# Two independent lanes for the side matrix products of an attention-and-GLU kernel: one PSUM bank and one queue for each half of the TensorE rows

## The chip, the cores and the metric

The kernel runs on one core of a Trainium2 chip. The metric is the device time of one execution in microseconds (us), the median of several runs. In the profile, PE is TensorE's matmul stream and PEld its weight loads, DVE is VectorE, ACT is ScalarE, POOL is GpSimd and SP is SyncE, which here only issues DMAs.

## What is computed

One transformer block over S = 2048 rows of width D = 512, with a modulation of its layer norms by a conditioning vector `c`. There are H = 32 query heads of width 16 that share one key and one value head (multi-query), and a GLU without a nonlinearity, of width F = 1792.

```
mod = (silu(c) @ w_mod)                      # six rows: sa, ca, ga, sb, cb, gb
h = layernorm(x) * (1 + ca) + sa
q = h @ wq  (32 heads of 16);  k = h @ wk;  v = h @ wv        # one k, one v
p = softmax(q k^T * 16**-0.5);  o = p v
x = x + ga * (o @ wo)
h = layernorm(x) * (1 + cb) + sb
x = x + gb * (((h @ w_gate) * (h @ w_up)) @ w_down)
```

All inputs and outputs are float32. Every product of float32 numbers on a float16 path is made of three float16 products: the left and the right operand are each split into a high and a low half, and high x high, low x high and high x low are accumulated (`TERMS`). An "operation" of a side product below is one such term for one slice of 128 of the contraction.

## The kernel before

**Steps.** The rows are four blocks (`NB`) of 512 queries. A block has 32 heads in 8 units of 4 heads, so there are 32 units (`NU`), and each unit has 32 steps (`NSTEP`): 1024 steps in a loop that is written out at build time. Every instruction stands in its engine's queue in the order in which the loop emits it.

**What a step does.** TensorE's 128 rows are used as two halves of 64 (parameter `a`, 0 or 1), and each half as four column quarters of 32, so that eight small matmuls can be in the array at a time. `quarters` (L521 is the full-width matmul of `plain`, L474 is the one in `quarters`) issues the four that fill one PSUM bank of 128 x 512. In a step with `a = i % 2` the loop emits, in this order (L1166 on): `max_half(a, 0, 2)`, scores of a later unit on half `a` (tile `mx`), whose row maximum DVE takes (L565); `qk_exp` on half `a` (tile `sc`), whose exponential ACT takes (L601); `pv` on the other half (L609, float32, each issued as two passes); then a second `max_half` and a second `qk_exp` on half `a`; then the side work. The maxima run 38 steps (`LEAD`) ahead of the scores, so the last 38 steps of the loop have none. `mx` has two banks, `sc` has two, and a third one (`spare`) while no side product needs it.

**Side products.** `q` of the later blocks, and, for each finished block, `wo`, the second layer norm, gate, up and down are done as side work between the attention matmuls. A `Group` is one output bank of 128 x 512: 12 operations for q, wo, gate and up, 42 for down. They go in pairs (`duo`): two groups, one in the bank `misc`, one in the bank `spare`. In a first turn the first group gets the upper half of each contraction slice on row half 0 while the second group gets the lower half on row half 1; in the second turn they change over, so that in both turns both halves work and no bank is written by both halves at once. Each operation of the generator is eight quarters, four on each half. Between the turns there is a pause of `SWAP_WAIT` = 2 steps, or, once the weights are all prepared, one step and a `memset` of a token on POOL (L498) that the second turn waits for. When the pair is done the first group is evicted at once and the second a step later (`mids`). After it there are `GROUP_WAIT` = 2 steps to the next pair.

**Pacing.** `pace` works out how many operations a step needs so that everything in the list `fill` is done by its due step (for a block's wo, gate, up and down: 12 steps into the next block but one); the sum is kept as `credit`, capped at 6, and `fill_gap` emits at most `BURST` = 3 operations in a step. In the last block `RESERVE / PAIR` = 142 operations may be left for the time after the loop, and a pair of downs isn't opened where fewer than 30 steps remain (`open_gate`).

**Evictions.** Gate is copied by ACT (L783), up by ACT (L790) and multiplied on POOL (L791), which also splits the product into halves (L794, L795). wo (L697) and down (L808) are scaled and added by one DVE operation each, and the layer-norm statistics follow on DVE (L705, L708).

**Weights.** While the first blocks run, a second list (`side`) streams each weight in slices twice: first for norms and scales (squares on POOL, L877, L879; column sums on PE, L889, their maxima on DVE, L892), at one slice per `ABS_GAP` = 2.5 steps, then for the float16 halves.

**After the loop** the remaining downs of block 2 are done with full 128 x 128 matmuls (`cover`), in the gaps of the last normalisation, then wo, the layer norm, gate, up and down of block 3, in the same way.

Of the kernel before, what the change touches and what calls it, by code (L numbers as in the profile page):

```python
# [21 lines left out]
NB = 4  # L22
# [6 lines left out]
ABS_GAP = 2.5  # L29
# [9 lines left out]
SWAP_WAIT = 2  # L39
RESERVE = 31000.0  # L40
TR_GAP = 8
BURST = 3
# [11 lines left out]
def adaln_mqa_glu_kernel(ctx: ExitStack, tc: tile.TileContext, x_in, wq_in, wk_in, wv_in, wo_in,  # L54
# [12 lines left out]
    spare = {"n": 0, "scores": True, "held": 0}  # L67
# [18 lines left out]
    def ps_misc(shape=(128, 512), dt=F32, tag=None):  # L86
        bufs = 1
        if tag is None:
            tag, bufs = ring["tags"][ring["n"] % len(ring["tags"])]
            ring["n"] += 1  # L90
        elif tag == "sc":
            bufs = NSC
        return psum.tile(list(shape), dt, name="misc", tag=tag, bufs=bufs)
# [9 lines left out]
    wqs = work.tile([128, KC, 64], F32, name="wqs", tag="xl", bufs=3)  # L103
# [14 lines left out]
    wqst = [work.tile([128, D], F32, name="wqst", tag=("gf", "oc")[k // 2], bufs=2) for k in range(KC)]  # L118
# [58 lines left out]
    modT = [consts.tile([128, KC, 64], F32, name=f"modT{i}") for i in range(2)]  # L177

    def mod_cols(row, dst, pt):
# [3 lines left out]
        nc.scalar.activation(dst[:, :, 0:32], pv_[:, :, 0:32], AF.Copy)  # L183
        nc.scalar.activation(dst[:, :, 32:64], pv_[:, :, 32:64], AF.Identity, bias=1.0)
# [56 lines left out]
    def ln_tr(b, ks=range(KC)):  # L241
        for k in ks:
# [4 lines left out]
            bias, scale = (hsb[:, k, 0:1], hsb[:, k, 1:2]) if b else (modT[0][:, k, 0:1], modT[0][:, k, 32:33])  # L247
# [47 lines left out]
    mrow = work.tile([128, 256], F32, name="modrow", tag="xl", bufs=3)  # L295
# [6 lines left out]
    nc.scalar.activation(modT[0][:, :, 32].rearrange("p (h c) -> p h c", c=2),  # L302
# [4 lines left out]
    nc.vector.tensor_reduce(cmk[:, 0:1], modT[0][:, :, 32], axis=AX.X, op=OP.max, apply_absolute_value=True)  # L307
# [39 lines left out]
    nc.vector.tensor_scalar(hsb, modT[0][:, :, 0:64:32], fwd[:, 0:1], None, op0=OP.mult)  # L347
# [103 lines left out]
    def v_evac():  # L451
        vt["v"] = work.tile([128, BT], F32, name="kvT", tag="ev", bufs=3)
        nc.scalar.activation(vt["v"], vt["p"], AF.Copy, scale=qvs[:, 1:2])
# [13 lines left out]
    class Group:  # L467


        def __init__(self, n, op, pre, post, mid=True):  # L470
            self.n, self.op, self.pre, self.post, self.mid = n, op, pre, post, mid
# [4 lines left out]

    def half(p, g, i, r, start, stop):
        left, right = g.op(i)
        return quarters(p, left[64 * r:64 * r + 64], right[64 * r:64 * r + 64], start, stop)

    token = consts.tile([1, 1], F32, name="token")
    SYNC = mybir.DependencyInfo(mybir.DependencyClass.Sync, mybir.DependencyReason.DATA)

    def duo(g0, g1, tags=("misc", "spare")):

        ps = g0.pre(tag=tags[0]), g1.pre(tag=tags[1])
        n = g0.n
        mark = None
        for turn in range(2):
            for i in range(n):  # L490
                for r in range(2):
                    ms = half(ps[r ^ turn], (g0, g1)[r ^ turn], i, r, turn == 0 and i == 0,
                              turn == 1 and i == n - 1)
                    if mark is not None:
                        tc.add_manual_dep(ms[0].ins, mark.ins.name, SYNC, reason="row halves of one bank in turn")
                        mark = None
                if turn == 0 and i == n - 1 and cur["mark"]:
                    mark = nc.gpsimd.memset(token, 0.0)  # L498
                    tc.add_manual_dep(mark.ins, ms[-1].ins.name, SYNC, reason="end of a row half")
                if turn == 0 or i < n - 1:  # L500
                    yield i == n - 1
        g0.post(ps[0])

        def late():
            g1.post(ps[1])
            after(3, free)

        def free():
            spare["held"] -= 1

        spare["held"] += 1
        if g1.mid:
            mids.append(late)
        else:
            after(2, late)
# [9 lines left out]

    def q_proj(b, ch):

        def evac(p):
            q16 = work.tile([128, 2, BT], F16, name="q16", tag="ev", bufs=3)
            qf = work.tile([128, BT], F32, name="qf", tag="ev", bufs=3)  # L530
            nc.scalar.activation(qf, p, AF.Copy, scale=qvs[:, 0:1])  # L531
            nc.gpsimd.tensor_scalar(q16[:, 0, :], qf, 1.0, 0.0, op0=OP.mult, op1=OP.add)
            nc.gpsimd.tensor_tensor(q16[:, 1, :], qf, q16[:, 0, :], op=OP.subtract)
            d = dram.tile([128, 2, BT], F16, name=f"qd{b}_{ch}")
            nc.sync.dma_start(d, q16)
# [7 lines left out]
        return Group(3 * KC, op, ps_misc, evac, mid=False)  # L543
# [29 lines left out]
    def max_rows(u):  # L573
# [5 lines left out]
        def g():  # L579
# [5 lines left out]
            for hl in range(2):  # L585
                nc.sync.dma_start(s[48 + hl:113 + hl:64, :, :], mt[hl])
# [27 lines left out]
    def pv_lower(u):  # L614
        evt[u] = work.tile([128, BT], F32, name="ev", tag="ev", bufs=3)
        nc.scalar.activation(evt[u], pvb[u, 0], AF.Copy, scale=evs)  # L616

    def pv_out(u):
# [7 lines left out]
        for j in range(4):  # L626
            r = 16 * (h + j)
            nc.sync.dma_start(oc[b, g // 2][r:r + 16, :], ev[32 * j:32 * j + 16, :])
        nc.sync.dma_start(rsum[b, g // 2][h:h + 4, :], ev[16:128:32, :])
# [494 lines left out]
    for n in range(LEAD):  # L1124
# [5 lines left out]
        if n in first:  # L1130
            first[n]()
# [145 lines left out]
```

## Time and profile before

| | |
|---|---|
| median of 3 runs | 1771.94 us (1771.19 to 1771.97) |
| the profiled execution's own time | 1771.55 us |
| its span in the profile | 1769.7 us, granted TensorE clock 0.994 |
| POOL busy | 562.5 us (32%) |
| matmuls / weight loads | 39203 / 39203 |
| DMA | 70.04 MB, 34 GB/s of HBM over the span |

The span runs from the first to the last instruction. A busy time is the union of an engine's instructions. A matmul's record begins when it enters the array, and its end is modelled, so matmuls overlap and PE's busy share says little; distances between the starts of matmuls on the same row half say more. "x" counts instructions. A side operation of the loop is eight matmul records, and a step has two exponentials (L601).

### The profile page before, as it was taken

What the parts mean: (1) busy time and instruction counts of PE and PEld (TensorE: products, weight loads), DVE (VectorE), ACT (ScalarE), POOL (GpSimd) and SP (SyncE); (2) the same over time, 40 slices, a digit from 0 to 9 for tenths busy, and PEclk for the clock granted to TensorE, in tenths of its full rate; (3) what the DMA queues carried; (4) which work ended last, traced back from release to release, by engine and by line L of the source; (5) the groups of instructions that cost most, each with busy time, mean ns of one, the idle gap of its engine ahead of it and who ended that gap; (6) DMA issues with size and microseconds to landing.
All of it is one profiled execution on the core that took longest, in us unless ns stands there. A gap on an engine that the chain in (4) does not pass through costs nothing. (4 is left out here: it accounts for less than half of the span.)

```text
span 1769.7 us, 86400 instructions
## 1 busy us (share of the span) xinstructions
PE 1707.4 (96%) x39203; PEld 878.6 (50%) x39203; DVE 1442.1 (81%) x2353; ACT 1301.8 (74%) x2319; POOL 562.5 (32%) x788
## 2 busy tenths in 40 slices
PE   6899999999999999999999999999999999999999
PEld 3334444433345565565545555565545555543444
DVE  7899999999998888899998888899999998922210
ACT  3478888878878878887788888887888888893110
POOL 5714444436657852210032222110032121221130
PEclk9999999999999999999999999999999999999999
DMA  5212222212222210000100000000100000001000
GB/s 195 100 32 80 60 80 62 77 46 73 80 74 58 66 34 15 11 19 23 42 23 18 11 10 20 7 16 24 48 16 18 12 18 11 14 7 41 19 0 24
DMA packets 49115, 70.04 MB, mean 40 GB/s; under 512 B 15270, under 2 KB 29418, under 8 KB 48748
## 3 DMA queue, kind: packets, MB, share of 16 engines
q1 hardware_dynamic: 47164, 64.33, 12.2%
q8 instruction: 306, 5.01, 1.2%
q14 instruction: 61, 0.50, 0.1%
q10 hardware_dynamic: 1584, 0.20, 0.1%
HBM read 51.12 MB, written 8.92 MB: 34 GB/s over the span
## 5 line engine op out<-in xcount | busy, mean ns | idle before, releaser
L565 DVE TENSOR_REDUCE mpart<-mx 128x1 f32<-128x512 f32 x2048 | 1329.0, 685 | 125.9 <-PE mx L474 36.1
L601 ACT ACTIVATE P<-sc 128x512 f32<-128x512 f32 x2048 | 1177.0, 601 | 259.9 <-PE sc L474 203.7
L609 PE MATMUL pv<-P,vst 64*32 64x512 f32 x8192 | 1080.8, 598 | 0.0
L474 PE MATMUL mx<-kst,sst 48*32 48x512 f16 x8192 | 808.4, 383 | 35.7 <-DVE mpart L565 27.2
L474 PE MATMUL sc<-sst,kst 50*32 50x512 f16 x8192 | 818.5, 379 | 5.3 <-ACT P L601 4.5
L474 PEld LDWEIGHTS <-sst 48*32 48x32 f16 x8192 | 335.6, 90 | 514.4 <-issue 420.9
L474 PEld LDWEIGHTS <-kst 50*32 50x32 f16 x8192 | 264.2, 92 | 92.7 <-issue 60.7
L474 PE MATMUL misc<-h2T,wu 64*32 64x512 f16 x4032 | 294.8, 376 | 0.0
L474 PE MATMUL misc<-h2T,wg 64*32 64x512 f16 x4032 | 294.2, 376 | 0.0
L609 PEld LDWEIGHTS pv<-P,vst 64*32 64x32 f32 x8192 | 197.8, 105 | 17.9 <-ACT P L601 0.8
L791 POOL TENSOR_TENSOR gf<-gf,g 128x512 f32<-128x512 f32 x42 | 53.7, 1279 | 344.2 <-ACT gf L790 344.2
L474 PEld LDWEIGHTS <-wu 64*32 64x32 f16 x4032 | 111.0, 92 | 36.1
L474 PEld LDWEIGHTS <-wg 64*32 64x32 f16 x4032 | 112.9, 92 | 30.7 <-issue 1.5
L474 PE MATMUL misc<-wd,glu 64*32 64x512 f16 x2688 | 112.9, 376 | 0.0
L474 PE MATMUL misc<-h,wq 64*32 64x512 f16 x1536 | 95.4, 377 | 1.2 <-ACT qf L531 1.2
L498 POOL MEMSET token<- 1x1 f32 x43 | 3.8, 88 | 281.4 <-PE misc L474 216.7
L783 ACT ACTIVATE g<-misc 128x512 f32<-128x512 f32 x56 | 33.4, 596 | 77.0 <-PE misc L521 75.5
L521 PE MATMUL misc<-wd,glu 128*128 128x512 f16 x336 | 73.2, 379 | 0.0
L474 PEld LDWEIGHTS <-glu 64*32 64x32 f16 x2688 | 60.3, 92 | 23.4 <-issue 0.4
L795 POOL TENSOR_TENSOR glu<-gf,glu 128x512 f16<-128x512 f32 x56 | 65.0, 1161 | 4.7
L793 DVE TENSOR_TENSOR gf<-misc,g 128x512 f32<-128x512 f32 x14 | 9.7, 692 | 62.9 <-PE misc L521 62.9
L621 DVE SCALAR_TENSOR_TENSOR ev<-pv,evs,ev 128x512 f32<-128x512 f32 x32 | 23.7, 742 | 44.5 <-ACT ev L616 44.5
(232 smaller groups left out, 1063.1 us busy)
## 6 DMA issues: line engine op xcount, KB each, us to landing
wsl<-in_B_w_gate_dram SPq DMA_DIRECT2D x32, 224.0 KB
wsl<-in_B_w_up_dram SPq DMA_DIRECT2D x32, 224.0 KB
wsl<-in_B_w_down_dram SPq DMA_DIRECT2D x28, 256.0 KB
sst<-qd SPq DMA_DIRECT2D x186, 32.0 KB
qd<-q SPq DMA_DIRECT2D x16, 256.0 KB
oc<-ev SPq DMA_DIRECT2D x128, 32.0 KB
rr<-ri SPq DMA_DIRECT2D x16, 256.0 KB
xl<-in_A_x_dram SPq DMA_DIRECT2D x16, 256.0 KB
```

Source lines behind the costliest of these rows:

```text
L474: return [nc.tensor.matmul(p[c:c + CW, :], left[:, c:c + CW], right, start=start, stop=stop) for c in range(0, 128, CW)]
L498: mark = nc.gpsimd.memset(token, 0.0)
L521: nc.tensor.matmul(p, left, right, start=i == 0, stop=i == g.n - 1)
L565: nc.vector.tensor_reduce(mparts[u][:, a, p, t, kc:kc + 1], m, axis=AX.X, op=OP.max)
L601: nc.scalar.activation(ptl[u, kt, a][:, p, :], t, AF.Exp)
L609: nc.tensor.matmul(pvb[u, r][32 * j:32 * j + 32, :], vst[ks, kt, :], ptl[u, kt, a][ks, p, :], start=(kt == 0), stop=(kt == KT - 1))
L621: nc.vector.scalar_tensor_tensor(ev, pvb[u, 1], evs, ev, op0=OP.mult, op1=OP.add)
L783: nc.scalar.activation(st["g", f], p, AF.Copy, scale=2.0 ** -45)
L791: nc.gpsimd.tensor_tensor(gf, gf, st["g", f], op=OP.mult)
L793: nc.vector.tensor_tensor(gf, p, st["g", f], op=OP.mult)
L795: nc.gpsimd.tensor_tensor(st["glu"][:, 1, f, :], gf, st["glu"][:, 0, f, :], op=OP.subtract)
```

## The change

- Each row half becomes a `Lane`, with its own bank (`misc` or `spare`), its own queue `todo`, its own credit, and its own waits. `duo`, the turns, the pause between them and the token are gone.
- Gate and up: a group is done by one lane alone. It has 24 half operations (4 quarters each) instead of 12 whole ones, since both halves of each contraction slice go through the same 64 rows. For that the weights are stored with the halves of the rows exchanged as slices 4 to 7 (`2 * KC`), loaded by two DMAs for each slice, and h2 is copied with its halves exchanged by two DMAs (SBUF to SBUF) for each of its four slices. Lane 0 has the first seven columns of F / 128, lane 1 the last seven.
- q, wo (blocks 0 to 2) and down (blocks 0 to 2): each lane makes a partial sum over its own 64 rows in its own bank. Both are evicted, and added: q by a second ACT copy and a POOL add; wo by an ACT copy of the one and the DVE operation for the other, and a POOL add of x; down by an ACT copy and a POOL add each, with none on DVE.
- A lane emits `min(int(credit), BURST, left)` half operations in a step, `BURST` = 4; one of the lane `a` ahead of the second `max_half`, then all of the other lane, then the rest of `a`. A lane waits with a new group while the other one is in the first third of one of the same length, unless its credit is full.
- The transposes of h2 are dealt to the lanes in turn, and gate and up open 4 steps after the last of them (`H2_WAIT`).
- The remaining 142 operations of `RESERVE` are counted in each lane, and there is no gate that keeps a down group from opening late. After the loop the lanes go on in turn (`pair`), with two banks each; block 3's gate and up are done so too.
- Weights: `ABS_GAP` 2.0; the squares of wo and down on ACT, with the sum in the same operation, and half of those of gate and up on ACT; fewer, wider column sums.
- Smaller: the DMAs of the maxima's rows (`mt`) are issued by ACT, several DMAs are issued one to four steps later than their data, `ev` has four buffers.

```diff
-    def duo(g0, g1, tags=("misc", "spare")):
-        ps = g0.pre(tag=tags[0]), g1.pre(tag=tags[1])
-        for turn in range(2):
-            for i in range(n):
-                for r in range(2):
-                    ms = half(ps[r ^ turn], (g0, g1)[r ^ turn], i, r, turn == 0 and i == 0,
-                              turn == 1 and i == n - 1)
...
+    def rows_of(op, a):
+        def f(i):
+            left, right = op(i)
+            return left[64 * a:64 * a + 64], right[64 * a:64 * a + 64]
+        return f
...
     def q_proj(b, ch):
         def evac(p):
+            t = work.tile([128, BT], F32, name="qf", tag="ev", bufs=NEV)
+            nc.scalar.activation(t, p, AF.Copy, scale=qvs[:, 0:1])
+            if "t" not in st:
+                st["t"] = t
+                return
+            nc.gpsimd.tensor_tensor(t, t, st["t"], op=OP.add)
...
+            def send():
+                for hl in range(2):
+                    nc.scalar.dma_start(s[48 + hl:113 + hl:64, :, :], mt[hl])
+            after(1, send)
...
         def fin(t):                                   # wo
+                elif (b, t) not in x1s:
+                    x1 = x1s[b, t] = work.tile([128, D], F32, name="x1", tag="x1", bufs=4)
+                    nc.scalar.activation(x1, p, AF.Copy, scale=sca[:, 7:8])
+                    return
                 else:
+                    nc.vector.scalar_tensor_tensor(x1, p, sca[:, 7:8], x1, op0=OP.mult, op1=OP.add)
+                    nc.gpsimd.tensor_tensor(x1, x1, xls[b, t], op=OP.add)
...
+                def send():                           # h2, halves exchanged
+                    for a in range(2):
+                        nc.sync.dma_start(h[64 * a:64 * a + 64, :, KC + k, :], h[64 - 64 * a:128 - 64 * a, :, k, :])
+                after(2, send)
...
         def fin(t):                                   # down
-                nc.vector.scalar_tensor_tensor(o, p, sca[:, 6:7], o, op0=OP.mult, op1=OP.add)
+                    y = turns()
+                    nc.scalar.activation(y, p, AF.Copy, scale=sca[:, 6:7])
+                    nc.gpsimd.tensor_tensor(o, o, y, op=OP.add)
...
+        gu = [[Group(6 * KC, op(a, f, w), pre, (gate, up)[w](FT // 2 * a + f)) for f in range(FT // 2) for w in range(2)]
+              for a in range(2)]
...
+        def plan(self, step):
+            self.credit = min(self.credit + self.pace(step), CREDIT)
+            if self.credit < 1.0:
+                return 0
+            if self.g is None:
+                if not self.opens(step):
+                    return 0
...
+                other = lanes[1 - self.r]
+                if other.g and other.g.n == self.todo[0][1].n and other.i < other.g.n // 3 and self.credit < CREDIT:
+                    return 0
+                self.begin()
+            return min(int(self.credit), BURST, self.left())
...
             drain_mids()
+            first_n = min(ns[a], 1)
+            side_half(step, a, first_n)
             max_half(a, 1, 2)
             qk_exp(u, kt, 1, a)
...
+            side_half(step, 1 - a, ns[1 - a])
+            side_half(step, a, ns[a] - first_n)
```

More of the change, by code (lines that the diff above doesn't have):

```diff
@@ L117, in adaln_mqa_glu_kernel @@
         nc.gpsimd.memset(w, 0.0)
-    wqst = [work.tile([128, D], F32, name="wqst", tag=("gf", "oc")[k // 2], bufs=2) for k in range(KC)]
+    wqst = [work.tile([128, D], F32, name="wqst", tag=("ev", "oc")[k // 2], bufs=(NEV, 2)[k // 2]) for k in range(KC)]
     for k in range(KC):
@@ L787, in fn @@
             def fn(p):
-                gf = work.tile([128, BT], F32, name="gf", tag="gf", bufs=2)
+                gf = turns()
                 if b < NB - 1:
@@ L1093, in begin @@
-    def begin(step, two, due, tags=("misc", "spare")):
-        cur.update(gen=duo(*two, tags=tags), left=2 * two[0].n, turn=two[0].n, second=False, due=due, swapped=-9,
-                   mark=not side)
-    def burst(step, n):
-        for _ in range(n):
-            swap = next(cur["gen"], None)
-            credit[0] -= 1.0
-            cur["left"] -= 1
-            cur["turn"] -= 1
-            if swap is None:
-                cur["gen"], cur["left"], cur["wait"] = None, 0, step + GROUP_WAIT
-                return
-            if swap:
-                cur["turn"], cur["second"], cur["swapped"] = cur["left"], True, step
-                return
+    END = NU * NSTEP
@@ L1110, in adaln_mqa_glu_kernel, with side_half, free @@
+    lanes = [Lane(0, "misc"), Lane(1, "spare")]
+    def side_half(step, l, n):
+        if n:
+            done = lanes[l].emit(n)
+            if done:
+                lanes[l].wait = step + GROUP_WAIT
+                lanes[l].held += 1
+                def free():
+                    lanes[l].held -= 1
+                mids.append(done)
+                after(4, free)
     side_next = [0.0]
@@ L1145, in adaln_mqa_glu_kernel @@
             posts.append(v_out)
-    assert cur["gen"] is None
-    for two in qtwos:
-        fill.append(([0, 0], "duo", two, QDUE))
-    credit[0] = 0.0
-    def ffn_twos(b):
-        gu, down = ffn_work(b)
-        return gu + twos(down)
+    assert lanes[0].g is None and lanes[1].g is None
+    for lane in lanes:
+        lane.credit, lane.wait = 0.0, 0
     early["on"] = False
@@ L1163, in adaln_mqa_glu_kernel @@
             drain_posts()
-            spare["scores"] = not spare["held"] and cur["gen"] is None and not (fill and fill[0][1] == "duo" and open_gate(step))
             a = p
+            ns = [lane.plan(step) for lane in lanes]
+            spare["scores"] = not lanes[1].held and lanes[1].g is None and not lanes[1].opens(step)
             max_half(a, 0, 2)
@@ L1219, in adaln_mqa_glu_kernel, with pair @@
     pv_out(u)
-    left = cur["left"]
-    if cur["gen"] is not None:
-        assert cur["second"] and NU * NSTEP - cur["swapped"] > 2
-        for _ in cur["gen"]:
-            drain_posts()
-        drain_mids()
-    ring["tags"] = [("misc", 1), ("spare", 1)] + [("mx", NMX)] * NMX + [("sc", NSC)] * NSC
-    tail = deque(plain(g) for _, _, two, _ in fill for g in two)
+    drain_mids()
+    ring["tags"] = [("mx", NMX)] * NMX + [("sc", NSC)] * NSC
+    banks = [deque(("misc", "pv")), deque(("spare", "pvb"))]
+    def pair():
+        some = False
+        drain_posts()
+        for lane, tags in zip(lanes, banks):
+            if lane.g is None and lane.todo:
+                lane.tag = tags[0]
+                tags.rotate(-1)
+                lane.begin()
+            if lane.g:
+                some = True
+                done = lane.emit(1)
+                if done:
+                    done()
+        return some
     def cover(budget):
-        while tail and budget > 0:
-            drain_posts()
-            if next(tail[0], None) is None:
-                tail.popleft()
+        while budget > 0 and pair():
             budget -= 216
@@ L1254, in adaln_mqa_glu_kernel @@
     gu, down = ffn_work(NB - 1)
-    run([g for two in gu for g in two] + down)
+    for lane, gs in zip(lanes, gu):
+        lane.todo.extend(([0], g, 0) for g in gs)
+    cover(1e9)
+    run(down)
 _INS = ["A_x", "A_wq", "A_wk", "A_wv", "A_wo", "B_w_gate", "B_w_up", "B_w_down", "c", "w_mod"]
```

372 lines of the change are left out of this document (200 added, 172 removed).

## The prediction, made before the change was run

> **What bounds it now.** I read the page first, then the table of windows by stage (all instructions, then only the exponentials of L601, then only those on tile `misc`), then the timeline.
>
> ```profile
> PE 1707.4 (96%) x39203; PEld 878.6 (50%) x39203; DVE 1442.1 (81%) x2353; ACT 1301.8 (74%) x2319; POOL 562.5 (32%) x788
> ...
> L565 DVE TENSOR_REDUCE mpart<-mx 128x1 f32<-128x512 f32 x2048 | 1329.0, 685 | 125.9 <-PE mx L474 36.1
> ```
>
> PE's 96% is a union of overlapping records. DVE's row maxima alone are 1329 us, 685 ns each, two in a step. Now the stages: q only (93 to 456), the two stretches of gate, up and first downs (542, 934), end of downs, wo and layer norm (846), the last long stretch (1323).
>
> ```profile
> 93.00:456.00 363.00, 349.32 (x7607) 146.53 (x7607) 340.18 (x567) 307.72 (x541) 160.95 (x174) 0.99 0.22 63
> ...
> 542.00:846.00 304.00, 300.01 (x8531) 181.47 (x8530) 270.75 (x424) 243.09 (x440) 111.83 (x125) 1.00 0.12 31
> 846.00:934.00 88.00, 84.75 (x2062) 43.96 (x2049) 81.50 (x133) 70.36 (x125) 17.93 (x45) 0.98 0.11 32
> 934.00:1237.00 303.00, 300.54 (x8555) 179.78 (x8546) 270.48 (x425) 243.97 (x441) 53.45 (x67) 1.00 0.06 15
> ...
> 1323.00:1559.00 236.00, 233.40 (x6265) 129.06 (x6254) 214.32 (x341) 199.68 (x359) 50.53 (x62) 1.00 0.06 14
> ```
> ```profile
> 93.00:456.00 363.00, 296.56 (x512) 0.99 0.22 63
> ...
> 542.00:846.00 304.00, 228.07 (x399) 1.00 0.12 31
> ...
> 1323.00:1559.00 236.00, 186.71 (x324) 1.00 0.06 14
> ```
> ```profile
> 542.00:846.00 304.00, 155.91 (x3748) 0.00 (x0) 1.48 (x2) 16.89 (x28) 1.00 0.12 31
> ...
> 1323.00:1559.00 236.00, 111.95 (x2388) 0.42 (x4) 0.00 (x0) 15.26 (x25) 1.00 0.06 14
> ```
>
> Two exponentials make a step. With q only there are 256 steps of 363/256 = 1.418 us, and DVE is busy 340.18/363 = 93.7%: DVE sets the step, and I take 93.7% for what a DVE-bound stretch reaches. From 846 on it is 92.6%: DVE again. From 542 on there are 199.5 steps of 1.524 us with 3748/8/199.5 = 2.35 side operations each and DVE at 89.1%; the stretch at 934 is the same. From 1323 on: 162 steps of 1.457 us, 1.84 operations, DVE 90.8%. There PE is late as well. The timeline of PE says how:
>
> ```profile
> 668.25 0.60 PE L609 MATMUL pv<-P,vst 64*32 64x512 f32 x4
> 668.42 0.40 PE L474 MATMUL mx<-kst,sst 48*32 48x512 f16 x4
> 668.64 0.40 PE L474 MATMUL sc<-sst,kst 50*32 50x512 f16 x4
> 668.68 0.60 PE L609 MATMUL pv<-P,vst 64*32 64x512 f32 x4
> 668.86 0.40 PE L474 MATMUL mx<-kst,sst 48*32 48x512 f16 x4
> ...
> 670.65 0.40 PE L474 MATMUL misc<-h2T,wg 64*32 64x512 f16 x4
> 670.80 0.40 PE L474 MATMUL misc<-h2T,wu 64*32 64x512 f16 x4
> 670.87 0.40 PE L474 MATMUL misc<-h2T,wg 64*32 64x512 f16 x4
> ...
> 671.30 0.61 PE L609 MATMUL pv<-P,vst 64*32 64x512 f32 x4
> 671.45 0.40 PE L474 MATMUL mx<-kst,sst 48*32 48x512 f16 x4
> 671.67 0.40 PE L474 MATMUL sc<-sst,kst 50*32 50x512 f16 x4
> ```
>
> On one row half four quarters follow four quarters after 0.22 us (mx 668.42, sc 668.64, mx 668.86; wg 670.65, 670.87), and a pass of pv holds the other half 0.43 us (668.25, 668.68). So a step with n operations on a half needs 0.217 x (4 + n) us: 1.30 for 2, 1.52 for 3. At 2.35 it is 1.38 on average, below DVE's 270.75/199.5/0.937 = 1.45. The 1.52 measured comes from unevenness: steps of 3 are set by PE at 1.52, empty and light ones by DVE, and pairs end badly:
>
> ```profile
> 663.94 0.59 ACT L783 ACTIVATE g<-misc 128x512 f32<-128x512 f32 x1
> ...
> 664.89 0.62 ACT L790 ACTIVATE gf<-misc 128x512 f32<-128x512 f32 x1
> ...
> 665.08 0.40 PE L474 MATMUL sc<-sst,kst 50*32 50x512 f16 x4
> ...
> 665.52 0.40 PE L474 MATMUL mx<-kst,sst 48*32 48x512 f16 x4
> ...
> 666.05 0.40 PE L474 MATMUL sc<-sst,kst 50*32 50x512 f16 x4
> ```
>
> Gate and up are evicted within a step, the exponentials on ACT slip, and PE's next sc, mx, sc stand 0.44 and 0.53 us apart instead of 0.22, with no side work in between: 0.53 us lost per pair.
>
> **The change, part by part.**
>
> *Lanes in the loop.* The operations per half are the same (a 24-operation group on one lane for 12 on both, twice). Gone are the turn, its pause and the token; gate and up end in different steps, so ACT gets one 0.6 us eviction at a time. New is that the halves carry different n. Working the rule of `plan` through for a gate-up stretch (2.38 per step and lane, one empty step after each group, then up to 4 from the saved credit) gives steps such as [0,2] [4,2] [3,0] [2,4] [3,4] [2,2] [3,3]; the larger of the two averages 2.9, with 2, 3 and 4 about equally often. No trace shows unequal halves, so I bound it from both sides. *Elastic*: a half works ahead while the other is late, the five steps above cost each half 0.867 x 5 + 0.217 x 12 = 6.94 us, DVE is the bound, and the stretches fall to DVE busy/0.937: 289, 289 and 229 us, that is -15, -14 and -7 = -36. *Lockstep*: each step costs the larger half, max(1.45, 0.217 x (4 + n)): thirds of 1.45, 1.52 and 1.74 average 1.57 where equal halves (by the old rule 0, 3, 3, 3, 3, 3, 2, 3, 2, 2 for 24) give 1.49; 0.08 less 0.02 for the halved pile-up is +0.06 x 400 = +26, and 0.04 x 162 = +7 in the last stretch, where the larger of the two averages 2.3: +33. I take -15, nearer to the elastic end, for this row: pv is queued behind mx and sc of its step (L1166, L1167, L1170), yet at 671.30 it starts 0.15 us before that mx and 0.37 us before that sc. A half does run past the other by 0.37 us, and the unevenness to be hidden is two operations, 0.43 us.
>
> The Trainium skill speaks against this: "TensorE: Matmul & The Clock Gate", section "The mechanism", states that matmuls keep program order in start and end, a strict FIFO without reordering. By that rule the blocks of one lane and then the other would run one after the other, and the sum would be that of the third rival below; the row at 671.30 differs from it, and the measurement decides.
>
> *The end.*
>
> ```profile
> 1593.78 11.91 ACT L601 ACTIVATE P<-sc 128x512 f32<-128x512 f32 x24
> ```
> ```profile
> 1662.04 2.75 PE L521 MATMUL misc<-h2T,wg 128*128 128x512 f16 x12
> ...
> 1664.63 2.75 PE L521 MATMUL misc<-h2T,wu 128*128 128x512 f16 x12
> ```
> ```profile
> L521 PE MATMUL misc<-wd,glu 128*128 128x512 f16 x336 | 73.2, 379 | 0.0
> ```
>
> After the loop 12 operations take 2.59 us (1662.04 to 1664.63 on one engine with nothing else): 0.216 each. Of the 336 full-width downs 168 are block 3's, so all 168 of block 2's are left over, as no pair opens in the last 30 steps. By the new rule a lane has three groups, 126, left: 42 x 0.216 = -9. They go into the loop's last steps, where ACT sets 2 x 11.91/24 = 0.99 us and a half needs on average (0.434 + 0.867)/2 = 0.65: 1.6 operations a step are free, the rule emits 3.5 over 12 steps, so about 20 cost 0.217: +4. Sum -5; bounds -9 and 0. The lanes' eight quarters per 0.217 us are what the loop's threes do already.
>
> *DVE.*
>
> ```profile
> L531 ACT ACTIVATE qf<-misc,qvs 128x512 f32<-128x512 f32 x16 | 11.1, 691 | 4.3 <-PE mx L474 2.3 <-POOL q L533 2.0
> ...
> L808 DVE SCALAR_TENSOR_TENSOR x<-misc,sca,x 128x512 f32<-128x512 f32 x12 | 8.9, 744 | 21.3 <-PE misc L521 21.3
> ...
> L892 DVE TENSOR_REDUCE cmq<-mx 128x1 f32<-128x128 f32 (+1 forms) x16 | 4.4, 274 | 0.3 <-PE mx L889 0.3
> ```
>
> Eight of the twelve down additions (blocks 0 and 1) leave DVE in stretches that it sets: 8 x 0.744 = -6. Of sixteen column maxima four, wider, remain: 4.4 us less an estimated 1.6 = -3; taken together as -8. wo keeps one DVE operation per group.
>
> *ACT and POOL.*
>
> ```profile
> L791 POOL TENSOR_TENSOR gf<-gf,g 128x512 f32<-128x512 f32 x42 | 53.7, 1279 | 344.2 <-ACT gf L790 344.2
> ...
> L377 ACT ACTIVATE wqj<-wqst 128x512 f32<-128x512 f32 x4 | 2.5, 628 | 0.1
> ```
> ```profile
> 1.73 0.53 ACTq L104 DMA_DIRECT2D wqs<-in_A_wq_dram  x1
> ```
>
> Added to ACT in the q stretch: 14 second q copies x 0.69 = 10, 34 squares at 0.55 to 0.63 plus sums = 22, and 16 DMA issues (an issue by ACT took 0.53) = 8: 40 us onto 307.72 of 363. It fits only because exponentials in a row take 0.50, not the 0.58 that they average there; so ACT is late more often. Later stages get a copy per wo and down group, and 0.53 x 2 per unit. I take +4, bounds 0 and +15; a gain is excluded, as ACT only gets more. POOL loses the squares and gains adds of 1.28 us (as L791); at 160.95 of 363 nobody waits for it, except bn_stats on DVE, which comes three steps (4.5 us) after wo's eviction: if POOL is later than that, the row maxima queue behind it, up to 1.3 x 12 = 15 us. The exchanged copies of h2 have 4 steps, 6 us, and stand in SP's queue; while they travel DVE sets the step, so nothing. If they are late, PE's queue stops at operation 13 of the first groups, scores and all, some 2 us per block.
>
> Sum: -15 - 5 - 8 + 4 = -24 on the profiled execution's 1771.55 (the median of the runs is 0.4 higher): 1748 us.
>
> **Rivals.**
>
> *Fully elastic.* -36 - 5 - 8 + 0 = -49: 1722 us. For it: passes of pv start ahead. Against: mx waits for DVE in a queue that stops at a wait, and all behind it wait too, whichever half they are for.
>
> *Lockstep (slower).* The place is the gate-up stretches: where a half cannot run more than one operation ahead, each 4 against 2 costs its step 0.43 us. +33 - 5 - 8 + 8 = +28: 1800 us; it decides against the change as soon as less than half of the unevenness is hidden. For it: the threes at 1.52 show no step that borrows from its neighbour. Against: 671.30.
>
> *Strict order (slower).* No start overtakes another: then of each step's operations those of the second lane begin after the last of the first, (2.35 - 1) x 0.217 = 0.29 us x 400 and 0.18 x 162: +146, about 1900 us. Only the row at 671.30 speaks to it, clearly against.
>
> *Nothing to win.* Both lanes open gate and up in the same step (full credit passes the stagger), evictions fall together as now, and the halves' -5 and -8 are eaten by ACT: 1769 to 1775 us.
>
> **Numbers.** Forecast 0.48, fully elastic 0.22, nothing 0.10, lockstep 0.17, strict order 0.03. A change of 0.2%, 3.5 us, is about what can be told from none. Faster 0.70, same 0.10, slower 0.20. The range 1712 to 1788 takes in the elastic case with the ACT term and column maxima at their better ends, and the lockstep case up to half hidden plus the late ACT.
>
> **What would show it.** The windows by stage: gate-up stretches at about 1.48 us a step and DVE near 92%; no L498; starts of one half's quarters several operations ahead of the other's; 126 pairs after the loop and 156 us for all behind it; q stage unchanged within 5 us. I am wrong if the gate-up step is over 1.52, if DVE's idle time is ended by `misc` or `sc` on PE more than now, if bn_stats waits for POOL, or if the q stage grows.

## The result and the profile after

The changed kernel takes 1813.92 us (1809.59 to 1816.01, four runs) against 1771.57 us: a ratio of 1.0236 (1.0217 to 1.0256). It is slower, by 42 us, and outside the predicted range. Its profiled execution took 1813.35 us, with a span of 1811.5 us.

The page of the changed kernel, busy times and the row of the maxima (L540 is what was L565):

```profile
PE 1732.2 (96%) x42637; PEld 930.3 (51%) x42637; DVE 1431.2 (79%) x2331; ACT 1361.3 (75%) x2423; POOL 575.9 (32%) x752
...
L540 DVE TENSOR_REDUCE mpart<-mx 128x1 f32<-128x512 f32 x2048 | 1327.4, 686 | 164.6 <-PE sc L477 87.8
```

DVE has about the same work (1431 for 1442 us) in a longer span. Its idle time ahead of the maxima grew from 125.9 to 164.6 us, and most of that now ends with a score matmul on PE. ACT is busy 60 us longer, and PE has 3434 more matmuls.

The windows by stage of the changed kernel, all instructions, for the stretch with q only and for 304 us that begin 17 us behind the start of the first gate and up stretch (the table further down compares the stretches themselves); then the same two windows for the exponentials alone (L580):

```profile
93.00:456.00 363.00, 341.61 (x7088) 145.19 (x7085) 316.95 (x521) 308.45 (x569) 171.48 (x199) 0.98 0.27 75
...
586.00:890.00 304.00, 302.24 (x8626) 190.38 (x8630) 269.30 (x422) 252.22 (x444) 59.48 (x57) 1.00 0.07 17
```
```profile
93.00:456.00 363.00, 274.64 (x474) 0.98 0.27 75
586.00:890.00 304.00, 235.95 (x400) 1.00 0.07 17
```

In the first window 474 exponentials make 237 steps of 1.53 us, where there were 256 of 1.42. DVE is busy 317 us of 363 instead of 340, and ACT 308 as before, but for 19 steps fewer: 1.30 us a step for 1.20. In the second, 200 steps of 1.52 us: what it was before.

To compare the kernels step by step I took the start of the first score matmul of each step from the trace and added up between fixed steps. All times in us; 0 to 192 is most of the q stage, 313 to 512, 569 to 768 and 825 to 986 are the three gate, up and down stretches, 986 to 1024 the steps without maxima.

| steps | ahead | 0-192 | 192-313 | 313-512 | 512-569 | 569-768 | 768-825 | 825-986 | 986-1024 | behind |
|---|---|---|---|---|---|---|---|---|---|---|
| before | 93.3 | 269.9 | 178.7 | 304.3 | 88.1 | 302.7 | 85.9 | 236.0 | 45.4 | 165.4 |
| after | 94.8 | 294.9 | 178.8 | 304.4 | 89.4 | 304.4 | 90.9 | 235.7 | 52.9 | 165.2 |
| e1 | 95.3 | 288.6 | 178.6 | 302.0 | 89.3 | 302.6 | 89.3 | 234.7 | 52.5 | 164.7 |
| e5 | 95.2 | 277.5 | 179.7 | 301.8 | 89.3 | 301.8 | 92.0 | 234.5 | 52.5 | 161.6 |
| e9 | 97.0 | 275.6 | 175.0 | 301.7 | 88.3 | 301.5 | 87.2 | 233.5 | 50.6 | 158.7 |

Of the 42 us lost, 25 lie in the first 192 steps, 7.5 in the last 38, and 5 in the steps 768 to 825. The three stretches, from which the prediction took 15 us in all, did not move. The waits of the changed kernel from 96 to 380 us say who is late (waiting engine and line, releaser, us in total, times, longest):

```profile
POOL kwb L910 <- ACT wsl L906: 24.9, 10, 8.7
...
DVE mpart L540 <- PE sc L477: 21.1, 48, 1.7
PE sc L477 <- ACT P L580: 7.6, 18, 1.2
```

and the same waits before:

```profile
DVE mpart L565 <- PE sc L474: 3.6, 8, 0.9
...
PE sc L474 <- ACT P L601: 1.3, 7, 0.2
```

The rows fit one chain: an exponential is late, the next score waits for its bank, the maxima's matmul stands behind the score in PE's queue, and DVE waits for it. They do not show that every wait is of this kind: DVE waits 48 times behind a score, and in 18 cases the score is seen to wait for an exponential. The timeline of the changed kernel shows the longest case, which ends just behind that window:

```profile
379.78 1.19 ACT L580 ACTIVATE P<-sc 128x512 f32<-128x512 f32 x2 [0.66 <-PE sc L477]
...
380.44 4.42 ACTq L563 DMA_DIRECT2D sst<-mt  x2
...
384.90 1.08 ACT L580 ACTIVATE P<-sc 128x512 f32<-128x512 f32 x2 [3.93 <-DMA wsl<-in_B_w_up_dram]
...
385.55 0.62 PE L477 MATMUL sc<-sst,kst 50*32 50x512 f16 x4 [3.53 <-ACT P L580]
385.56 1.08 PE L588 MATMUL pv<-P,vst 64*32 64x512 f32 x4
385.93 0.67 PE L477 MATMUL misc<-h,wq 64*32 64x512 f16 x4
```

ACT issues the two DMAs of the `mt` rows, and for 3.93 us no exponential runs. Each issue takes 0.52 us; between them the queue waits, as the second starts 3.9 us after the first. The profile names a landing weight slice as what ended the wait, and the trace says why: the second issue reports to the same semaphore as a slice of `w_up` that SP had issued at 381.82, and waits for that one first. PE stands for 3.53 us, and behind the pause its matmuls have durations of 0.62 to 0.67 instead of 0.40 us, while the granted clock is 0.50 (385.5 to 391 us).

### The profile page after: what moved, and what is told of

It is laid out like the page before. It is cut to its first block, busy times and chain, and to the rows that moved or that the text cites. A ratio compares the mean times of both kernels' runs of the same rounds, so it can differ in the third digit from the quotient of the medians.

```text
span 1811.5 us, 93282 instructions
## 1 busy us (share of the span) xinstructions
PE 1732.2 (96%) x42637; PEld 930.3 (51%) x42637; DVE 1431.2 (79%) x2331; ACT 1361.3 (75%) x2423; POOL 575.9 (32%) x752
## 4 chain that ended last, share of the span: by engine, by line
PE 80%; ACT 6%; DVE 6%; POOL 3%; issue 3%; DMA 2%; SPq 0%; ACTq 0%; DVEq 0%; POOLq 0%
PE misc L477 27%; PE pv L588 22%; PE mx L477 13%; PE sc L477 13%; ACT P L580 4%; DVE mpart L540 4%; PE misc L484 3%; DVE ev L600 1%; POOL h L405 1%; DMA wmA<-in_w_mod_dram 1%; ACT qf L501 0%; POOL h2T L744 0%; DMA sst<-qd 0%; PE misc L262 0%; ACT wsl L901 0%
## 5 line engine op out<-in xcount | busy, mean ns | idle before, releaser
L540 DVE TENSOR_REDUCE mpart<-mx 128x1 f32<-128x512 f32 x2048 | 1327.4, 686 | 164.6 <-PE sc L477 87.8
L580 ACT ACTIVATE P<-sc 128x512 f32<-128x512 f32 x2048 | 1196.3, 599 | 246.8 <-PE sc L477 186.6
L477 PE MATMUL sc<-sst,kst 50*32 50x512 f16 x8192 | 825.0, 379 | 24.9 <-ACT P L580 18.5
L477 PEld LDWEIGHTS <-sst 48*32 48x32 f16 x8192 | 319.9, 91 | 422.0 <-issue 286.4
L477 PEld LDWEIGHTS <-kst 50*32 50x32 f16 x8192 | 282.0, 92 | 146.2 <-issue 91.4
L797 POOL TENSOR_TENSOR glu<-glu,g 128x512 f32<-128x512 f32 x42 | 53.8, 1281 | 513.5 <-ACT glu L796 513.5
L477 PE MATMUL misc<-wd,glu 64*32 64x512 f16 x4032 | 204.0, 376 | 0.0
L477 PE MATMUL misc<-h,wq 64*32 64x512 f16 x1536 | 133.6, 382 | 0.5 <-ACT qf L501 0.5
L477 PEld LDWEIGHTS <-glu 64*32 64x32 f16 x4032 | 98.3, 92 | 42.6 <-issue 3.8
L819 POOL TENSOR_TENSOR x<-x,glu 128x512 f32<-128x512 f32 x24 | 30.7, 1280 | 205.5 <-ACT glu L818 204.9
L789 ACT ACTIVATE g<-misc 128x512 f32<-128x512 f32 x56 | 32.3, 596 | 64.5 <-PE misc L477 60.4
L477 PE MATMUL misc<-wo,och 64*32 64x512 f16 x1152 | 70.0, 381 | 0.0
L801 POOL TENSOR_TENSOR glu<-glu 128x512 f16<-128x512 f32 x56 | 65.1, 1163 | 4.7
```

The source lines that it names most:

```text
L477: return [nc.tensor.matmul(p[c:c + CW, :], left[:, c:c + CW], right, start=start, stop=stop) for c in range(0, 128, CW)]
L540: nc.vector.tensor_reduce(mparts[u][:, a, p, t, kc:kc + 1], m, axis=AX.X, op=OP.max)
L580: nc.scalar.activation(ptl[u, kt, a][:, p, :], t, AF.Exp)
L789: nc.scalar.activation(st["g", f], p, AF.Copy, scale=2.0 ** -45)
L797: nc.gpsimd.tensor_tensor(gf, gf, st["g", f], op=OP.mult)
L801: nc.gpsimd.tensor_tensor(st["glu"][:, 1, f, :], gf, st["glu"][:, 0, f, :], op=OP.subtract)
```

## The experiments

Each edit is against the kernel after, unless it says otherwise. Ratios are to the kernel before, with a 95% interval.

### Which added work on ACT costs

Theory A: the `mt` rows' DMAs on ACT. Rival A1: the weight stream (its pace, and its squares on ACT). Rival A2: the second q eviction.

**e1_mt_sp**

```diff
-                    nc.scalar.dma_start(s[48 + hl:113 + hl:64, :, :], mt[hl])
+                    nc.sync.dma_start(s[48 + hl:113 + hl:64, :, :], mt[hl])
```

> The changed kernel with the two DMAs of the maxima's rows issued by SP again instead of ACT, still a step after their data. Theory A (ACT is in the way: whatever holds ACT up makes PE's queue stop at the next sc, and DVE behind it): the 64 issues of 0.52 us and the stops between them go, about -15 us of 1814, in the steps behind each unit's maxima (the 30th of a unit falls from 1.97 to about 1.45 us). Theory B (the loss comes from halves of the array that carry unequal work): less than 3 us.

1798.29 us, 1.0145 (1.0128 to 1.0162): 15.6 us less. Theory A holds. The edit is worth almost four times the whole ACT term of the prediction. In the traces all of it lies in the last three steps of the units, where the DMAs were issued: these lose 14.3 us, the loop as a whole 13.9. The long wait is only part of it: of the 32 pairs of issues one more had such a wait (second issue 2.2 us after the first), the other pairs followed each other after 0.6 us, but for two of 1.2 and 0.9. The three units around the two long waits (the fifth to the seventh) lose 7.3 us by the edit, the other 29 together 6.6.

**e2_squares_pool**: the squares of the weight slices all on POOL again, at the new pace of 2.0 steps.

```diff
-            if m > 1:
-                nc.scalar.activation(t, t, AF.Square, accum_out=fro[:, m - 2, i:i + 1])
-                return
...
+            nc.gpsimd.tensor_tensor(to, t, t, op=OP.mult)
```

> The changed kernel with all 50 squares of the weight stream on POOL again; those of wo and down are added up on POOL and summed by one DVE operation each. Theory A: the first 128 steps lose about 8 of the 16 us that they are over the kernel before, the rest unchanged, 1806. Theory B: unchanged within 3 us.

1815.43 us, 1.0243 (1.0227 to 1.0258): no gain. Step by step it is a gain and two losses. Of the first 192 steps, those at a column sum on PE (89 to 92) lose 3.9 us and the last four of each unit, with the `mt` DMAs, 5.2; all others together win 7.8. In its waits from 96 to 380 us the column sums wait for POOL, which has no such row in the changed kernel:

```profile
PE mx L914 <- POOL kwb L904: 2.2, 2, 1.5
```

**e5_weights_as_before**: e1, and the squares on POOL, and also the old pace, `ABS_GAP = 2.5`, with two steps for a column sum.

> The changed kernel with the maxima's rows sent by SP, all squares of the weight stream on POOL (those of wo and down summed up there, one DVE sum each), a slice each 2.5 steps and 2 steps for a column sum, so that the weight stream runs as in the kernel before. Theory A1 (the faster stream with its squares on ACT costs the first 192 steps): of the 19 us by which they are still over the kernel before, 10 or more go, to about 1788. Theory A2 (the second copies of q do): 3 us or less go, 1796.

1786.91 us, 1.0086 (1.0071 to 1.0101): 11.4 us less than e1, and 11.1 of it in the first 192 steps. The weight stream costs; at the faster pace neither engine hides it. How much of the 11 us is the pace, the squares or the time for a column sum was not tried one by one.

**e6_lane1_later**: e1, and lane 1's evictions of q and wo two steps later.

> The changed kernel with the maxima's rows sent by SP, and the eviction of lane 1's q and wo groups two steps later than lane 0's, with two more steps before lane 1's next group. Theory A2 (two copies in one step hold up ACT for 1.4 us, and PE stops at sc): each of the 14 pairs of q costs about 0.5 us less, -7 us in the first 192 steps, 1791. Theory A1: within 2 us of 1798.

1808.23 us, 1.0205 (1.0188 to 1.0222). The first 192 steps lost only 1.6 us, so two q evictions in one step are not the matter; the gate and up stretches grew by 7 to 9 us; the shift also moves the lanes' phase against each other, which by itself was not tried.

**e11_before_mt_act**: the kernel before, with nothing but the `mt` rows' DMAs on ACT, a step later.

> Before, with one edit: the mt rows' 64 DMAs are issued by ScalarE one step later instead of by SP. If the cost of that edit is its own and not one of the half rows, 10 to 16 us on before: about 1785, most of it in the q stage, with a stall where a unit's scores wait for a weight slice. If it costs only beside the half rows, 1772.

1781.50 us, 1.0051 (1.0035 to 1.0067): 9 us slower, but spread over the stages, with only 3 us in the first 192 steps. The edit costs of itself, less than beside the rest. The long waits are missing here: no second issue starts more than about 1.2 us after the first, and the fifth to the seventh unit lose 1.5 us where e1 gave back 7.3.

**e12_before_weights**: the kernel before, with the weight stream's pace and squares.

> Before, with the weight stream of after: a gap of 2.0 steps between slices, and the squares of wo, down and the odd slices of gate and up on ScalarE. If the cost of that is its own, 8 to 12 us on before: about 1782, in the first 192 steps. If it costs only beside the half rows' evictions, 1772.

1792.04 us, 1.0114 (1.0096 to 1.0132): 20 us slower, more than expected; 15 of it in the first 192 steps, 6 in the next 121. It is not quite the changed kernel's stream: there ACT also adds up the squares of wo and down, and the column sums are fewer and wider; here POOL adds them all. So POOL's sums wait for ACT's squares still more (the waits from 93 to 380 us; 24.9 us in the changed kernel):

```profile
POOL kwb L883 <- ACT wsl L879: 73.6, 26, 22.0
```

Neither cost needs the lanes. Both are prices of the things that came along with them, though the 20 us are not the same as the 11 of e5.

### Which way the halves run

**e3_equal**: no stagger rule, so that both lanes mostly emit the same number in a step.

```diff
-                if other.g and other.g.n == self.todo[0][1].n and other.i < other.g.n // 3 and self.credit < CREDIT:
-                    return 0
```

> The changed kernel without the rule that a lane waits while the other is in the first third of a like group: both lanes then plan the same number in every step and end their groups together. Theory B: the gate-up stretches fall from 1.525 to about 1.48 us a step, -15 to -20 us. Theory A: evictions fall together again, so no gain, 0 to +6 us.

1820.61 us, 1.0273 (1.0256 to 1.029): 7 us slower than after. Steps with 4 and 4 half operations, most of which open a group on both lanes, take 2.3 us (19 of them in the steps 316 to 454). Here and below the half operations of a step are counted by the kernel's own plan.

**e4_alternate**: behind the second scores the lanes' half operations are emitted by turns instead of one lane after the other.

> The changed kernel with the side operations at the end of a step emitted by turns, one of the other lane, one of lane a, instead of all of the one and then all of the other. If starts are held to the order of the queue to some depth (theory C), the gate-up stretches gain 10 us or more; if the halves overtake each other freely, nothing (within 3 us). Theory A: nothing.

1810.81 us, 1.0217 (1.02 to 1.0235): no difference that can be told. The order in PE's queue within a step does not matter, so strict order is out, and so is lockstep as the prediction priced it: in e9 below, where a lane has at most 3, the steps with 5 half operations average 1.44 us over the steps 316 to 454, and those with 4 average 1.41. Lockstep had 1.52 for a 3 against a 2.

**e8_equal_late**: e1 and e3, lane 1's evictions a step later, and one more empty step after every group.

> The changed kernel with the maxima's rows sent by SP, with equal numbers on both lanes in every step (no staggering), and lane 1's evictions a step after lane 0's, with one more step between groups. Theory B (unequal halves cost the gate-up stretches what the apart evictions win): the two stretches fall from 302 to about 295 us each and the whole by 10 to 15 us against 1798. If unequal numbers cost nothing: 300 us or more each, from the additional empty step.

1816.06 us, 1.025 (1.0235 to 1.0265), with stretches of 310 us: parting the evictions this way wins nothing.

### The end

**e7_wide_tail**: e1, and the gate and up of block 3 behind the loop as 64x128 matmuls, one in place of four quarters.

```diff
-                quarters(self.p, left, right, self.i == 0, self.i == self.g.n - 1)
+                if wide[0]:
+                    nc.tensor.matmul(self.p, left, right, start=self.i == 0, stop=self.i == self.g.n - 1)
...
```

> The changed kernel with the maxima's rows sent by SP, and with block 3's gate and up, behind the loop, as one matmul of 64 rows by 128 columns for each half operation instead of four of 32 columns: the same products in the same order of lanes with a quarter of the instructions. Theory D (behind the loop PE runs out of instructions: it stops every 256 of them): the stops of 0.3 to 0.5 us go, -5 to -6 us. If the array's use is what costs, no change.

1792.99 us, 1.012 (1.0105 to 1.0135): 5.3 us less than e1. What it took away stands in the timeline of the changed kernel behind the loop:

```profile
1709.45 0.40 PE L477 MATMUL misc<-h2T,wu 64*32 64x512 f16 x7
1710.22 3.65 PE L477 MATMUL misc<-h2T,wu 64*32 64x512 f16 x128 [0.38 <-issue]
1714.24 1.88 PE L477 MATMUL misc<-h2T,wu 64*32 64x512 f16 x57 [0.38 <-issue]
```

PE stops for 0.38 us after 128 matmuls, each with its weight load: 256 instructions. From 1692.5 to 1771.2 us there are 15 such stops, always a multiple of 128 matmuls apart and of two lengths, 0.38 and 0.10 us in the profile's idle time for all but the first; at 6 more such multiples there is none. The starts across them are 0.41 to 0.76 us apart where 0.22 is usual, about 5 us in all, which is what e7 gave back. The instruction queue of the page has one packet for 256 instructions:

```profile
q8 instruction: 333, 5.46, 1.3%
```

2 x 42637 / 256 is 333. The Trainium skill, "Runtime: NRT & Kernel Launch", section "Instruction fetch mechanics", gives such blocks of 256 instructions, 16 KiB each, and calls the cost of crossing one mostly hidden. The packets agree; here, where nothing but quarters runs, it is hidden at 6 of 21 crossings. The pairs of gate and up behind the loop took 78.7 us (1692.5 to 1771.2) for 336 pairs, and with one matmul for four, 336 x 0.216 = 72.6.

**e10_all_wide**: e5, and every half operation as one 64x128 matmul, in the loop too. That is a quarter of the instructions of the side work (the text on record says half).

> After, with the mt rows' DMAs on SP and the weight stream as before, and every pair of half operations of a lane issued as one 64x128 matmul, in the loop and behind it: half the TensorE instructions of the side work. If the number of instructions holds the gate and up stretches at 302 us, they lose 10 us and more each: about 1760. If it does not, only the end gains its 5 us: 1782. If a 64x128 matmul cannot run beside the two half-row chains of the other kind, the stretches grow: 1790 and more.

2585.49 us, 1.4577 (1.4545 to 1.4609). A gate and up stretch took 489 us, 2.46 a step. The timeline:

```profile
960.08 0.61 PE L588 MATMUL pv<-P,vst 64*32 64x512 f32 x4
960.62 0.39 PE L1148 MATMUL misc<-h2T,wu 64*128 64x512 f16 x1
960.94 0.40 PE L477 MATMUL mx<-kst,sst 48*32 48x512 f16 x4
961.16 0.39 PE L477 MATMUL sc<-sst,kst 50*32 50x512 f16 x4
961.48 0.61 PE L1148 MATMUL misc<-h2T,wu 64*128 64x512 f16 x4
962.02 0.40 PE L477 MATMUL mx<-kst,sst 48*32 48x512 f16 x4
```

Before and behind every 64x128 matmul stand 0.32 us where quarters follow each other in 0.22, and no start of the other half falls between. The third case of the expectation came out, far beyond its size. The Trainium skill, "TensorEngine Tiling (Array Packing)", section "Tiling Modes", says that a change of the tiling mode drains the array; the rows agree.

### Bursts, and where the stretches' gain went

**e9_burst3**: e5 and e7, and `BURST = 3` instead of 4.

> After, with the mt rows' DMAs on SP, the weight stream's squares, gaps and column sums as before, the gate and up behind the loop as 64x128 matmuls (the edits that were worth about 16, 11 and 5 us), and at most 3 half operations of one step and lane instead of 4. Without the last edit the three add up to about 1782 us. If steps with 4 or more half operations are what eats the shorter lanes' gain in the gate and up stretches, each of the two stretches loses another 3 to 5 us: about 1774. If the stretches are held by the step's chain, 1782 and stretches of 302.

1770.67 us, 0.9993 (0.9984 to 1.0003): level with the kernel before. e5 less the 5.3 us of e7 would be 1781.6, so by this difference of runs the bursts cost 11 us. But not in the gate and up stretches, which stay at 301.7 and 301.5. Most of it lies between them: steps 192 to 313 and 768 to 825 are each about 5 us shorter than in e5. Both named outcomes missed this one. With the gains of e1, e5 and e7, 15.6, 11.4 and 5.3 us, that is 43, about the 42 us that the change lost.

The timeline of e9 shows part of what is left in a stretch, in its worst form. Both lanes' banks are evicted (L789), then both lanes open a group with `wu`:

```profile
715.26 0.40 PE L477 MATMUL sc<-sst,kst 50*32 50x512 f16 x4
715.60 1.08 ACT L789 ACTIVATE g<-misc 128x512 f32<-128x512 f32 x2
...
716.55 1.71 ACT L580 ACTIVATE P<-sc 128x512 f32<-128x512 f32 x3
716.73 0.40 PE L477 MATMUL misc<-h2T,wu 64*32 64x512 f16 x4
716.95 0.40 PE L477 MATMUL mx<-kst,sst 48*32 48x512 f16 x4
717.22 0.40 PE L477 MATMUL sc<-sst,kst 50*32 50x512 f16 x4
717.23 0.83 PE L477 MATMUL misc<-h2T,wu 64*32 64x512 f16 x20
717.39 0.69 DVE L540 TENSOR_REDUCE mpart<-mx 128x1 f32<-128x512 f32 x1 [0.40 <-PE mx L477]
...
718.33 0.69 DVE L540 TENSOR_REDUCE mpart<-mx 128x1 f32<-128x512 f32 x1 [0.25 <-PE mx L477]
```

The first `wu` starts as the evictions end, the maxima of the step stand behind it in PE's queue, and DVE waits. That step takes 2.25 us. In the steps 316 to 454, 3 open a group on both lanes and take 2.29 us on average, and 10 open one beside three half operations of the other lane and take 1.86. Three edits of e9 were meant to take the wait away, and a fourth asks the same of the kernel before.

**e13_evict_early**

```diff
             drain_posts()
+            drain_mids()
             a = p
...
-            drain_mids()
             first_n = min(ns[a], 1)
```

> e9_burst3 with one edit: the copy that frees a lane's bank is emitted at the head of the next step, ahead of its exponentials, not in the middle. If the gate and up stretches are held by the first half operation of a new group, which waits for its bank and stops scores and maxima behind it, the steps that open a group fall from 1.9-2.3 to about 1.5 us: 20 openings a stretch at 0.4 us, stretches of about 294 and the whole at 1750 to 1758. If ScalarE's load holds them: 1770, stretches of 302.

**e14_wait3**: `GROUP_WAIT = 3`.

> e9_burst3 with GROUP_WAIT 3 instead of 2: a new group opens one step later. If the wait for the bank holds the stretches: the opening steps fall to about 1.5 us, stretches of 290 to 296, though more steps have three half operations on both lanes; the whole 1750 to 1762. If unevenness costs as in the case of halves that run in step, the stretches grow to 305 and more.

**e15_side_last**: `first_n = 0`.

> e9_burst3 with all side half operations behind the step's second maxima and scores; none ahead. If what costs is that the first half operation of a group waits for its bank in front of the second maxima: the opening steps fall by 0.3 to 0.5 us, stretches of about 295, the whole at 1755 to 1762. If the half operation ahead filled time in which the half would be idle: slower, 1775 to 1785.

**e16_before_wait3**: the kernel before with `GROUP_WAIT = 3`.

> Before, with GROUP_WAIT 3 instead of 2. There too the step after a pair of gate and up takes 1.87 us, and its first operation waits for the copy of up. If that is the same wait for the bank, each gate and up stretch loses 4 to 7 us, 1760 to 1766 in all, if the later opening can be made up; if the lost step has to be made up by steps of three, 1772 to 1778.

None gained: 1774.60 (1.0014, 1.0005 to 1.0023), 1800.39 (1.0157, 1.0141 to 1.0172), 1784.37 (1.0062, 1.0047 to 1.0077) and 1776.45 (1.0024, 1.0014 to 1.0033). In e13 the opening step fell from 2.25 to 1.76 us as expected, and the step ahead of it rose from 1.26 to 1.99. Its timeline, same group:

```profile
718.17 1.08 ACT L789 ACTIVATE g<-misc 128x512 f32<-128x512 f32 x2
...
719.12 1.77 ACT L580 ACTIVATE P<-sc 128x512 f32<-128x512 f32 x3
719.79 0.40 PE L477 MATMUL sc<-sst,kst 50*32 50x512 f16 x4 [0.55 <-ACT P L580]
719.80 0.64 PE L588 MATMUL pv<-P,vst 64*32 64x512 f32 x4
720.01 0.40 PE L477 MATMUL misc<-h2T,wu 64*32 64x512 f16 x4
...
721.00 0.69 DVE L540 TENSOR_REDUCE mpart<-mx 128x1 f32<-128x512 f32 x1 [0.81 <-PE sc L477]
```

Now the bank is free in time, but the exponentials stand behind 1.08 us of evictions, the score waits for them, and DVE waits 0.81 us instead of 0.40 and 0.25. ACT's eviction is on the path in both places. In e14 the opening steps fell to 1.80 us, but 91 of the steps 316 to 454 have threes on both lanes instead of 63, and the 26 empty ones take 1.61 us. In e15 the opening steps did not fall: 2.25 us where both lanes open (2.29 in e9), and 2.06 instead of 1.86 where one opens beside three.

**e17_no_empty**: e13 and e15 together with `GROUP_WAIT = 1`, so that no step is left empty after a group. **e18_no_empty_ahead**: the same without e15.

> e9_burst3 with the eviction at the head of the next step, GROUP_WAIT 1 and all half operations behind the second maxima and scores, so that a new group opens in the step after the last one, behind its eviction. If the empty steps and the steps of three that make up for them hold the gate and up stretches: fewer steps of 3 + 3, stretches of 290 to 296, the whole 1750 to 1765. If they do not: stretches of 302 to 306 as in e15, 1775 to 1785.

> The same as e17, but one half operation of the step's own half stands ahead of the second maxima, as in the change. By the theory of the empty steps 290 to 298 a stretch, with some wait for the bank on half of the openings; 1750 to 1768 in all. Otherwise 302 and more, 1772 or above.

1777.85 us (1.0035, 1.0022 to 1.0047) and 1781.74 us (1.0057, 1.0042 to 1.0072), stretches of 303. In e17, steps with 6 half operations became fewer (30 of 139 for 63 of 139 in e9), steps with 5 took their place (66 for 25), and these now took 1.51 instead of 1.44 us: nothing won. The theory of the empty steps falls.

## Why the prediction was wrong

**ACT and POOL, "+4, bounds 0 and +15": this step failed, and it carries the sign.** The term was mis-sized: taking the `mt` DMAs off ACT gave back 15.6 us (e1), the old weight stream 11.4 more (e5), 27 us in all. The added busy time was right: without the issues the prediction's 40 us are 32, and ACT's instructions in the first 192 steps went from 241 to 274 us. What failed is the next link, that this "fits" into 363 us because exponentials in a row take 0.50 us. What costs is an exponential that comes late: with two score banks, a delay on ACT goes through PE's queue to DVE. For the `mt` DMAs the prediction took the duration of one issue, 0.53 us, which was right too (0.52), and no wait between two issues. That wait had no row before, and it came in two units of 32 (the longest at 380.44, two issues in 4.42 us). The issues were moved from SP, whose queue only issues DMAs, to the queue of the exponentials. The faster pace of the weight stream has no term in the prediction, and by e2 taking the squares off ACT at that pace does not give the 11.4 us back.

**Lanes in the loop, "I take -15": wrong, 0 in the changed kernel.** With all that was mended in e9 the three stretches lose 2.6, 1.2 and 2.5 us, 6 of the 36 of the elastic bound. The halves do run past each other, as the row at 671.30 said (e4; 3 and 2 cost no more than 2 and 2). What failed is the next link, that then "DVE is the bound, and the stretches fall to DVE busy/0.937". The unevenness that matters is not that between the halves of a step but that from step to step, and it hits both lanes: evictions by ACT, and threes on both lanes, 1.55 to 1.68 us on average over the steps 316 to 454, in every arrangement tried. The "pile-up" of 0.53 us a pair was seen rightly, but ending gate and up in different steps does not take it away: in the changed kernel a step with one eviction takes 1.65 us on average and one without 1.49 (27 and 112 of the steps 316 to 454).

**The end, "sum -5".** The last 38 steps grew by 7.5 instead of 4, and 42 fewer operations behind the loop should have brought 9, where the whole end stayed (165.4 to 165.2). "The lanes' eight quarters per 0.217 us are what the loop's threes do already" failed behind the loop: 78.7 us for 336 pairs instead of 72.6, most of it the instruction stops (e7 gave back 5.3). The other 3 us of the 9 stay open.

**Bursts.** The prediction counted steps of 4 only as lockstep in the gate and up stretches. They cost 11 us, elsewhere (e9, by the difference of runs given there).

**DVE, "-8 together".** The work left DVE (1442.1 to 1431.2 us), but the stage by stage sums do not show it apart. That the q stage would be "unchanged within 5 us" and that I would be wrong "if the q stage grows" was the sign that came: the first 192 steps grew by 25 us.

The rival that came nearest in time, lockstep at 1800, did so by luck: its place, the gate and up stretches, did not move. (Its 0.06 x 400 is 24 and not 26.)

Open: why a stretch stays at 301 to 306 us in e9, e13, e15 and e17, 1.51 to 1.54 us a step, though DVE needs 1.45 by the prediction's measure and each half 1.38. Part is seen in the 199 steps from 313 to 512 of e9. Six open a group on both lanes and take 2.30 us on average, 12 open one beside a three of the other lane and take 1.82, and 75 with threes on both lanes, which neither open nor end a group, take 1.57. Against 1.57 the openings cost 6 x 0.73 + 12 x 0.25 = 7 us, an estimate; the 75 threes are 9 us above DVE's 1.45, of which the 31 steps of two and two, at 1.33, give back 4. What holds the threes at 1.57 where the prediction has 1.52, and whether a stretch would fall without the evictions, was not tried.

No version tried beats the kernel before. In e9, with most of what came along taken back, the lanes are level with it: they win 6 us in the three stretches, 4 in the steps 192 to 313 and 7 behind the loop (5 of them by the wide matmuls), and lose 4 ahead of the loop, 6 in the first 192 steps and 5 in the last 38.

## What to carry to other kernels

Work added to an engine that is not the bottleneck, but feeds it through two buffers, has to be priced by how long it delays the next feeding each time, not by its busy time. A DMA issue holds its queue for as long as the wait that it meets (here 0.52 us, and up to 3.4 us more), so move one only to a queue that may stand. And when a change brings smaller edits along, predict each of them as if it came alone: here ACT's issues, the weight stream, bursts of four and quarters behind the loop made the 42 us.

## What the runs showed of the hardware

- Matmuls of 64x128 and of 64x32 do not share the array: each change between the two took 0.32 us where 0.22 would do, and nothing ran on the other half meanwhile (e10, 2.46 us a step).
- Quarters alone, 128 matmuls and as many weight loads in 3.65 us, run into a stop of 0.38 us (behind the loop of the changed kernel, where 15 of 21 blocks of 256 instructions ended in a stop, of 0.38 or of 0.10 us of idle time); 64x128 matmuls did not (e7).
- After PE had stood for 3.53 us, the same matmuls had durations of 0.62 to 0.67 us instead of 0.40, at a granted clock of 0.50 for about 5 us: the pause was paid for a second time. This is one case.
